# A fused lightning-attention and mixture kernel: values of one chunk with the scores of the next, the state decay on ScalarE, small constants in one tile, another order of the first loads

## Chip, cores and metric

The kernel runs on one core of a Trainium2 chip. The metric is the device time of one execution in microseconds (us); lower is better. Engines are named as in the profile: PE (TensorE matmuls), PEld (its weight loads), DVE (VectorE), ACT (ScalarE), POOL (GpSimd), and SP, whose queue issues most DMAs.

## The reference

First a lightning attention with decay, block by block; then its output, turned to one row per token, goes through four dense experts that are mixed by normalized domain probabilities.

```python
# q, k, v: (4, 8, 768, 64), lam: (8,), blocks of 64 tokens
for b in range(nb):
    intra = (q_b @ k_b.T * Dmask) @ v_b          # Dmask[i, j] = lam ** (i - j), i >= j
    inter = (q_b * lam ** (pos + 1)) @ kv_state
    out_b = intra + inter
    kv_state = lam ** 64 * kv_state + (k_b * lam ** (63 - pos)).T @ v_b
x = out.transpose(0, 2, 1, 3).reshape(3072, 512)
p = probs / (probs.sum(-1) + 1e-9)               # (3072, 4)
y = sum(p[:, e:e+1] * (relu(x @ w1[e]) @ w2[e]) for e in range(4))   # w1: 512x1024, w2: 1024x512
```

All of it is in fp32.

## The kernel before, in words

**Groups and chunks.** The tokens are cut into 24 chunks of 128 (two blocks of 64) with all 8 heads, and the chunks into three groups of 8, numbered 0 to 23. A group of 1024 tokens is what the experts work on. The attention of group 0 runs at the start, between the first expert products; the attention of groups 1 and 2 is spread through the expert products of the group before. `where(n)` gives a chunk its place in the sequence and its batch, and `after_of` the chunk that follows it in the same batch.

**The work of one chunk** is in four functions. `load` brings q, k and v in (SP's queue, L140). `turn` (L590) begins the state, scales k by the decay on POOL (`decayed`, L558), and transposes q and k on PE into two PSUM banks, copied out by ACT; chunks 16 to 23 "come across" instead, their q and k were already laid out in 32x32 blocks by DMAs, and DVE's transpose finishes them (`turn_across`, L575). `scores` (L617) does 32 matmuls of q against k (L633) and up to 32 of k against v for the state (L640), all of 64x64, into two banks `sp`. Three steps for DVE follow: the mask by the decay into `st`, the sum for the second block's state (`middle`), and `end`, which makes the state that the next chunk of the batch starts from: decay (`passed`, L490), then add. `values` (L669) does 32 matmuls of scaled q against the state (L687) and 32 of v against `st` (L705), also 64x64, into two banks, copied out by ACT (L726) with two adds on DVE. After every second chunk POOL makes `pair_sums` (L737), stored to DRAM in `x_blocks`, from which `x_fill` (L352) later refills the seven `xs` tiles of the next group.

**The expert products** are done by a two-level Strassen-like scheme with seven products M1 to M7 on each level. A unit is one group and one expert. In seven steps i of a unit the first product of the next unit (L974, banks g1 and g3, result `m`) and the second product of this unit (L1028, banks q01, q02, q11, q12, result `acc`) run interleaved. In each step the eight slots x hold, in turn, one part of the second product (eight PE matmuls) and two products of the first (four each); the last slot has one. Every bank is emptied by DVE or ACT, often followed by a Relu on ACT (L986).

**The order of work** is written out by hand. A counter `now` counts slots: slot = (unit * 7 + i) * 8 + x. `attention(g)` (L754) puts each chunk's load, turn, scores and values in slots by `BEGIN` (first slot and distance): group 1 turns chunks at 24 + 13i, group 2 at 152 + 22i; scores 4 slots later (6 for chunks that come across), values 10 (12) slots later. DVE work of a chunk goes into the list `lately`, of which one item is taken in each slot after that slot's products (`take`); a `values` forces what it needs of it. POOL's weight sums are `chores`, taken by a model of POOL's time; SP's stores follow from a queue. `FILL` gives the step from which `x_fill` refills one xs tile a step, in slot x = 3. All engines run their own instructions in program order.

**Group 0** has its own list of rows (L1436): turns, scores and values of chunks 0 to 7 (`ts`, `ss`, `vs`) between quarters of the products M1, M2 and M5 of the first unit (L1358), with the loads and POOL's weight sums S1 to S4 (`sum_first`) hung on rows.

**Memory.** Most tiles are 128x512 fp32 from one pool of `NPOOL` = 41 buffers (`small`). PSUM has eight banks: s0, s1 (attention), g1, g3 (first product), q01, q02, q11, q12 (second product). Small constants (`lam_bc`, `probs`, `gate`, `last_gate`, `total`, `decay`) have tiles of their own; of `decay` (128 x 8 x 128) rows 0 to 5 are in use in the attention, and the whole tile is overwritten by gates for the last group.

The lines that matter most:

```python
BEGIN = {1: (24, 13), 2: (8 * 19, 22)}                                        # L751
put(s + (6 if comes_across(n) else 4), lambda n=n: scores(n, ("s0", "s1")))   # L766
put(s + (12 if comes_across(n) else 10), lambda n=n: values(n, ("s0", "s1"))) # L767
tt(eng, o, s, q_decay[:, :, BL - 1:BL].to_broadcast([P, NHP, D]), ALU.mult)   # L491, passed
```

Of the kernel before, what the change touches and what calls it, by code (L numbers as in the profile page):

```python
# [14 lines left out]
FP32 = mybir.dt.float32  # L15
PSUM = bass.MemoryType.PSUM
DRAM = bass.MemoryType.DRAM
NPOOL = 41


@with_exitstack
def kernel(
# [69 lines left out]
    def small(name):  # L92
        return pool.tile([P, W], FP32, name=name, tag="t")
# [7 lines left out]
    def tt(eng, o, a, b, op):  # L101
        eng.tensor_tensor(out=o, in0=a, in1=b, op=op)  # L102
# [308 lines left out]
    def comes_across(n):  # L411
        return where(n)[0] >= SECOND
# [16 lines left out]
            load_across(n)  # L429
            load(n, "k")  # L430

    lam_bc = consts.tile([P, H], FP32, name="lam_bc")
    nc.scalar.dma_start(out=lam_bc[:], in_=lam.partition_broadcast(P))
    for n, names in ((0, "qk"), (1, "qk"), (0, "v"), (1, "v"), (2, "qk")):
        load(n, names)
    raw_w1(0, "A11")
# [21 lines left out]
    decay = consts.tile([P, CPG, P], FP32, name="decay")  # L458
    s_decay = decay[:, 0:4].rearrange("p (r x) (y i) -> p r (x y) i", r=2, i=BL)
    for r in range(2):  # L460
        for ac in range(NHP):
# [26 lines left out]
        tt(nc.vector, by_block(qs), by_block(of), by, ALU.mult)  # L488

    def passed(eng, o, s):  # L490
        tt(eng, o, s, q_decay[:, :, BL - 1:BL].to_broadcast([P, NHP, D]), ALU.mult)  # L491

    probs = consts.tile([P, NTOK // P, E], FP32, name="probs")
    gate = consts.tile([P, NTOK // P, E], FP32, name="gate")
    last_gate = consts.tile([P, CPG * E], FP32, name="last_gate")


    gate_rows = dram.tile([CPG, E, P], FP32, name="gate_rows")
    gate_bc = decay[:]

    def gates():
        total = consts.tile([P, NTOK // P], FP32, name="total")
        nc.vector.reduce_sum(out=total[:], in_=probs[:], axis=AX.X)
        nc.vector.tensor_scalar_add(out=total[:], in0=total[:], scalar1=1e-9)
        nc.vector.reciprocal(out=total[:], in_=total[:])
        nc.vector.tensor_tensor(
            out=gate[:], in0=probs[:], in1=total[:].unsqueeze(2).to_broadcast([P, NTOK // P, E]), op=ALU.mult,
        )

        for i in range(CPG):  # L510
            t = token(LAST, i // 4, i % 4) // P
            nc.vector.tensor_copy(out=last_gate[:, i * E:(i + 1) * E], in_=gate[:, t])

    def turn_gates():
        p, o = bank("s0", "gp"), small("gr")
        n = CPG * E
        nc.tensor.transpose(out=p[0:n, 0:P], in_=last_gate[:], identity=ident[:])
# [99 lines left out]
    def scores(n, tags):  # L617
        all_added()
        while n not in turned:
            take(lately, True)  # L620
        qT, kT = turned[n][0:2]
        while any(f in lately for f in turned[n][3:]):
            take(lately, True)
        begin_state(n)
        kd, vn = nat.pop((n, "kd")), nat[n, "v"]
        first, last = where(n)[0] == 0, where(n)[0] == NCH - 1

        sp = [bank(tags[r], "sp") for r in range(2)]
        blk = [slice(x * BL, (x + 1) * BL) for x in range(2)]
        for ac in range(NHP):  # L630
            for r in range(2):
                for x in range(2):
                    nc.tensor.matmul(  # L633
                        out=sp[r][half[x], ac * BL:(ac + 1) * BL], lhsT=hc(kT)[half[r], ac, blk[x]],
                        rhs=hc(qT)[half[r], ac, blk[x]], start=(ac == 0), stop=True, skip_group_check=True,
                    )
        for ac in range(NHP):
            for x in range(1 if last else 2):
                for r in range(2):
                    nc.tensor.matmul(  # L640
                        out=sp[x][half[r], 256 + ac * D:256 + (ac + 1) * D], lhsT=kd[half[x], 2 * ac + r],
                        rhs=vn[half[x], 4 * r + ac], start=False, stop=True, skip_group_check=True,
                    )
        st = small("st")
        added = [sp[x][:, 256:512].rearrange("p (h d) -> p h d", d=D) for x in range(2)]

        def mask(r):
            tt(
                nc.vector, st[:, r * 256:(r + 1) * 256], sp[r][:, 0:256], s_decay[:, r].rearrange("p h c -> p (h c)"),
                ALU.mult,  # L650
            )

        def middle():
            s = states[n][:, 1]
            if first:
                nc.scalar.copy(out=s, in_=added[0])
            else:
                tt(nc.vector, s, s, added[0], ALU.add)

        def end():  # L660
            s = states[after_of(n)] = small("kv")[:].rearrange("p (x h d) -> p x h d", x=2, d=D)
            passed(nc.vector, s[:, 0], states[n][:, 1])
            tt(nc.vector, s[:, 0], s[:, 0], added[1], ALU.add)

        work = [lambda: (mask(0), mask(1)), middle] + ([] if last else [end])
        soon(n, *work)
        masked[n] = st, work

# [78 lines left out]
            made.add(("blocks", g, x)),  # L747
        ))

    FILL = {1: 18, 2: 43}  # L750
    BEGIN = {1: (24, 13), 2: (8 * 19, 22)}  # L751
    steps = []

    def attention(g):  # L754

        def put(slot, f):
            steps.append((slot, f))

        for i in range(CPG):
            n, s = g * CPG + i, BEGIN[g][0] + BEGIN[g][1] * i  # L760
            put(s - 10, lambda n=n: load_more(n))
            put(s - 6, lambda n=n: load(n, "v"))
            put(s, lambda n=n: turn(n, ("s0", "s1")))
            if comes_across(n):
                put(s - 2, lambda n=n: (decayed(n), nat.pop((n, "k"))))
            put(s + (6 if comes_across(n) else 4), lambda n=n: scores(n, ("s0", "s1")))  # L766
            put(s + (12 if comes_across(n) else 10), lambda n=n: values(n, ("s0", "s1")))  # L767
            if n == 2 * CPG + 3:
                put(s + 17, turn_gates)
        steps.sort(key=lambda s: s[0])  # L770

    def forget():
# [240 lines left out]
    def second_product(g, e, m, banks):  # L1013

        def part(sj, s):
# [20 lines left out]
            if n not in acc:  # L1036
                acc[n] = acc_tile("acc"), set()
            a, begun = acc[n]
            o, x, w = a[:, j * DH:(j + 1) * DH], p[:, s * DH:(s + 1) * DH], gate[:, token(*where_of(n)) // P, e:e + 1]
# [384 lines left out]
        chores.extend((*prepare_w2(0), *(raw[n] for n in ("A11", "A22", "A21"))))  # L1424

    def load_probs():
        nc.scalar.dma_start(out=probs[:], in_=moe_domain_probs.rearrange("(t p) e -> p t e", p=P))

    def loads(*of):
        return lambda: [raw_w1(0, x) if isinstance(x, str) else load(x) for x in of]  # L1430
# [3 lines left out]

    h1, h2 = parts["M1"], parts["M2"]
    for f in (  # L1436
        (ts[0], lambda: warm(3)), (ts[1], lambda: warm(2)), (ss[0], loads(4, 5)), (ss[1], loads("A21", 6)),
        (vs[0], loads("A22")), (vs[1], loads(7)), (ts[2],), (m1[0],), (ss[2],), (m1[2],),
        (vs[2],), (ts[3],), (h2[0][0],), (ss[3],), (ts[4],), (h2[0][1],),
        (vs[3],), (h2[2][0],), (ss[4],), (ts[5],), (h2[2][1], sum_first("S3", "A11", "A21")),  # L1440
        (vs[4],), (h1[1][0],), (ss[5],), (ts[6], sum_first("S1", "A21", "A22", ALU.add)), (h1[1][1],),
        (vs[5],), (h1[3][0],), (ss[6],), (ts[7], load_probs), (h1[3][1], sum_first("S2", "S1", "A11")),
        (vs[6],), (h2[1][0], sum_x(0)), (ss[7],), (h2[1][1], sum_first("S4", "A12", "S2")),
        (begin_chores, m2[3]), (vs[7],), (sum_x(1), quarter_5(0)), (quarter_5(2),),
    ):
        for work in f:
            work()
        now[0] += 1
        pump()
# [178 lines left out]
```

## Time and profile before

| what | value |
|---|---|
| time, three runs | 1174.50, 1175.32, 1175.66 us, median 1175.32 |
| the profiled execution | 1171.55 us |
| its span, first to last instruction | 1169.8 us |
| granted TensorE clock | 1.000 |
| share of the span with PE busy | 99% |
| DVE, ACT, POOL busy | 68%, 23%, 55% |
| DMA moved | 255.63 MB, mean 219 GB/s |

A line of the timeline gives start, length, engine, source line, operation, output<-inputs, shape and count; brackets show idle time of the engine just before and what ended it. Matmuls overlap, and each has a modelled end, so times on PE are best read from start to start. An fp32 matmul of the program stands as two on PE, each with a weight load. A line of the list of waits gives the waiting engine and line, what it waited for, the sum, the number and the longest, in us.

### The profile page before, as it was taken

Reading aid. Unit: us, or ns where it says so; the run is one execution under the profiler, and the core shown is the slowest. Engines: PE = TensorE matmul, PEld = TensorE weight load, DVE = VectorE, ACT = ScalarE, POOL = GpSimd, SP = SyncE. Lnnn points to the kernel's source line nnn. Section 1 sums busy time; section 2 is a strip of 40 time slices with the busy share of each in tenths; the row PEclk is TensorE's granted clock in tenths of the full one; section 3 lists DMA queues with packets and bytes.
Section 4 is the critical chain, followed back from the end, with each engine's and each line's share of the span. In section 5 each row is a group of like instructions: output and inputs, shape, how many; then the busy total and the mean of one; then the engine's idle time right before and its main releaser. Section 6 shows DMA issues by size and latency. Waiting matters only on the chain.

```text
span 1169.8 us, 21185 instructions
## 1 busy us (share of the span) xinstructions
PE 1157.8 (99%) x8095; PEld 1006.5 (86%) x8095; DVE 791.7 (68%) x1407; ACT 271.1 (23%) x540; POOL 646.1 (55%) x640
## 2 busy tenths in 40 slices
PE   8999999999999999999999999999999999999998
PEld 7888888888888888888888888888888888888887
DVE  4666895578478567657747836745775666777785
ACT  4321122112211201211211120221233342341231
POOL 2846327546655761065245215655893683882884
PEclk9999999999999999999999999999999999999999
DMA  9884668998997996787868757785765445354442
GB/s 208 219 257 153 185 195 264 289 315 255 310 334 228 311 277 188 221 264 230 247 195 261 243 182 239 215 278 184 252 212 194 140 152 181 129 182 148 154 180 73
DMA packets 265717, 255.63 MB, mean 219 GB/s; under 512 B 121328, under 2 KB 219408, under 8 KB 265616
## 3 DMA queue, kind: packets, MB, share of 16 engines
q1 hardware_dynamic: 254976, 251.46, 69.0%
q10 hardware_dynamic: 10640, 2.82, 1.1%
q8 instruction: 64, 1.05, 0.4%
q14 instruction: 37, 0.30, 0.1%
HBM read 180.80 MB, written 77.61 MB: 221 GB/s over the span
## 4 chain that ended last, share of the span: by engine, by line
PE 95%; DVE 3%; POOL 1%; issue 0%; DMA 0%; ACTq 0%; ACT 0%; POOLq 0%; DVEq 0%
PE pg L974 39%; PE q L1028 31%; PE pq L1256 13%; PE pM L1358 2%; PE pc L1358 2%; DVE m L102 1%; PE sp L633 1%; PE op L687 1%; PE op L705 1%; PE sp L640 1%; PE qp L603 1%; PE kp L603 1%; POOL acc L102 1%; POOL m L102 1%; DVE sums L102 0%
## 5 line engine op out<-in xcount | busy, mean ns | idle before, releaser
L974 PE MATMUL pg<-xs,ws_in 128*128 128x256 f32 x1960 | 471.6, 380 | 0.8 <-DVE m L102 0.7
L1028 PE MATMUL q<-w2t,m 128*128 128x256 f32 x1792 | 424.4, 380 | 0.0
L974 PEld LDWEIGHTS pg<-xs,ws_in 128*128 128x128 f32 x1960 | 369.8, 190 | 53.7 <-DVE m L102 3.3
L102 DVE TENSOR_TENSOR m<-pg,m 128x512 f32<-128x512 f32 x451 | 307.2, 687 | 120.0 <-PE pg L974 109.8
L1028 PEld LDWEIGHTS q<-w2t,m 128*128 128x128 f32 x1792 | 339.3, 190 | 46.6 <-DVE m L102 0.4
L1046 DVE SCALAR_TENSOR_TENSOR acc<-q,gate,acc 128x256 f32<-128x256 f32 x192 | 92.3, 481 | 126.2 <-PE q L1028 125.7
L102 DVE TENSOR_TENSOR m<-m,m 128x512 f32<-128x512 f32 x184 | 152.5, 829 | 7.7 <-ACT m L986 7.7
L986 ACT ACTIVATE m<-m 128x512 f32<-128x512 f32 x132 | 83.0, 630 | 303.6 <-DVE m L102 302.5
L102 POOL TENSOR_TENSOR m<-m,decay 128x512 f32<-128x512 f32 x64 | 81.8, 1293 | 58.1 <-ACT m L986 44.7
L102 DVE TENSOR_TENSOR sums<-pq,sums 128x256 f32<-128x256 f32 x153 | 64.1, 421 | 45.7 <-PE pq L1256 36.9
L982 ACT COPY m<-pg 128x512 f32<-128x512 f32 x88 | 51.5, 585 | 186.1 <-PE pg L974 176.1
L1256 PE MATMUL pq<-acc,w2t 128*128 128x256 f32 x352 | 86.6, 379 | 0.0
L102 POOL TENSOR_TENSOR xs<-xs 128x256 f32<-128x256 f32 x56 | 44.5, 794 | 73.1 <-DMA xs<-x_blocks 57.4
L1256 PEld LDWEIGHTS pq<-acc,w2t 128*128 128x128 f32 x352 | 66.8, 190 | 9.3 <-issue 0.3
L102 POOL TENSOR_TENSOR to<-xc 128x256 f32<-128x256 f32 x16 | 12.5, 783 | 95.8 <-DVE xc L102 67.8
L102 POOL TENSOR_TENSOR acc<-hT,hT 128x512 f32<-128x512 f32 x32 | 40.2, 1269 | 29.7 <-PE pq L1256 27.8
L102 POOL TENSOR_TENSOR kn<-kn,decay 128x512 f32<-128x512 f32 x16 | 18.0, 1123 | 64.6 <-PE kp L603 43.7
L102 POOL TENSOR_TENSOR w2o<-w2b 128x512 f32<-128x512 f32 x32 | 42.4, 1348 | 18.3 <-DMA w2b<-in_moe_w_dram 10.2
L915 ACT ACTIVATE m<-m 128x512 f32<-128x512 f32 x44 | 27.7, 630 | 106.8 <-DVE m L102 106.8
L102 POOL TENSOR_TENSOR ops<-w2b 128x256 f32<-128x256 f32 x24 | 17.8, 764 | 50.7 <-issue 28.2
L102 POOL TENSOR_TENSOR acc<-hT,acc 128x512 f32<-128x512 f32 x32 | 40.7, 1271 | 7.4 <-PE pq L1256 5.4
L102 POOL TENSOR_TENSOR w2o<-w2b,w2o 128x512 f32<-128x512 f32 x24 | 34.2, 1449 | 5.8 <-issue 4.3
(135 smaller groups left out, 1204.8 us busy)
## 6 DMA issues: line engine op xcount, KB each, us to landing
ws_in<-w_ops SPq DMA_DIRECT2D x70, 896.0 KB, 6.3
w2t<-w_ops SPq DMA_DIRECT2D x66, 256.0 KB, 5.1
w2t<-w_sums SPq DMA_DIRECT2D x64, 256.0 KB, 3.7
w_ops<-ops SPq DMA_DIRECT2D x28, 512.0 KB, 4.3
w2t<-in_moe_w_dram SPq DMA_DIRECT2D x48, 256.0 KB, 3.6
w2b<-in_moe_w_dram SPq DMA_DIRECT2D x32, 256.0 KB, 5.5
w_sums<-w2o SPq DMA_DIRECT2D x16, 512.0 KB, 5.7
w2b<-in_moe_w_dram SPq DMA_DIRECT2D x16, 512.0 KB, 7.6
```

The source lines that it names most:

```text
L102: eng.tensor_tensor(out=o, in0=a, in1=b, op=op)
L603: nc.tensor.transpose(out=x[:, ac * C:(ac + 1) * C], in_=y[:, 2 * ac:2 * ac + 2].rearrange("p r d -> p (r d)"), identity=ident[:],)
L633: nc.tensor.matmul(out=sp[r][half[x], ac * BL:(ac + 1) * BL], lhsT=hc(kT)[half[r], ac, blk[x]], rhs=hc(qT)[half[r], ac, blk[x]], start=(ac ...
L640: nc.tensor.matmul(out=sp[x][half[r], 256 + ac * D:256 + (ac + 1) * D], lhsT=kd[half[x], 2 * ac + r], rhs=vn[half[x], 4 * r + ac], start=F ...
L915: nc.scalar.activation(out=o[:], in_=o[:], func=AF.Relu)
L974: nc.tensor.matmul(out=p[:, j * 256:(j + 1) * 256], lhsT=ws[i][:, j * P:(j + 1) * P], rhs=xs[i], start=(fresh and j == 0), stop=True, skip ...
L982: nc.scalar.copy(out=new[at][:], in_=p[:])
L986: nc.scalar.activation(out=new[at][:], in_=new[at][:], func=AF.Relu)
L1028: nc.tensor.matmul(out=p[:, s * DH:(s + 1) * DH], lhsT=h[A_OF[m]][:, c * 256 + s * P:c * 256 + (s + 1) * P], rhs=fed2[g, e, m][uu][:, c], ...
L1046: nc.vector.scalar_tensor_tensor(out=o, in0=x, scalar=w, in1=o, op0=ALU.mult, op1=ALU.add)
L1256: nc.tensor.matmul(out=p[:, 0:256], lhsT=fed3[e, m, x // 2][:, x % 2, c * P:(c + 1) * P], rhs=b[B_OF[i]][:, c * 256:(c + 1) * 256], start= ...
L1358: nc.tensor.matmul(out=p[:, s * 256:(s + 1) * 256], lhsT=a[c][:, f:f + P], rhs=b[:, c, j * 256:(j + 1) * 256], start=(s == 0 and c == 0 an ...
```

## The change

- **One step for two chunks.** In groups 1 and 2 eleven chunks (12 to 15 and 17 to 23) no longer have their scores alone: `both(n)` runs the values of chunk n-1, in banks s0 and s1, and then at once the scores of chunk n, in banks q02 and q12 of the second product. Chunks 8 to 11 and 16 keep a scores step of their own, and where no step for two follows (8, 9, 10, 15 and 23) values come six slots after the scores. `SCORES` lists the slot of each chunk's scores; the turn is 4 slots ahead (7 for chunks that come across), loads 10 and 6 slots ahead of the turn. `FILL` of group 1 goes from 18 to 19.
- **State decay on ScalarE.** From chunk 8 on `passed` is four ScalarE multiplications of 128x64 by a value per partition, in `end` (there on DVE before) and where a chunk begins (on POOL before).
- **Buffers.** From chunk 8 on the masked scores are written over `kT`; chunks that come across are scaled in place and after their scores. `probs`, `lam_bc`, `last_gate`, `total` and the gates as computed lie in rows 6 and 7 of `decay`; `gate` is kept for two groups, in chunk order, filled by 16 more copies of 128x4. `NPOOL` is 42.
- **First loads.** In group 0's rows chunks 6 and 7 are loaded ahead of the weight blocks A21 and A22, and POOL's sums S1 to S4 come in the later rows, S1 first, with `begin_chores` one row earlier.

```diff
-NPOOL = 41
+NPOOL = 42
...
-    lam_bc = consts.tile([P, H], FP32, name="lam_bc")
+    decay = consts.tile([P, CPG, P], FP32, name="decay")
+    lam_bc = decay[:, 6, 120:128]
...
     def passed(eng, o, s):
+        if eng is nc.scalar:
+            for ac in range(NHP):
+                nc.scalar.mul(out=o[:, ac], in_=s[:, ac], mul=q_decay[:, ac, BL - 1:BL])
+            return
         tt(eng, o, s, q_decay[:, :, BL - 1:BL].to_broadcast([P, NHP, D]), ALU.mult)
...
-        for i in range(CPG):
-            t = token(LAST, i // 4, i % 4) // P
-            nc.vector.tensor_copy(out=last_gate[:, i * E:(i + 1) * E], in_=gate[:, t])
+        for n in range(NG * CPG):
+            t = token(*where_of(n)) // P
+            to = gate[:, n] if n < LAST * CPG else last_gate[:, n % CPG * E:(n % CPG + 1) * E]
+            nc.vector.tensor_copy(out=to, in_=gates_of[:, t])
...
-            passed(nc.gpsimd, states[n][:, 1], states[n][:, 0])
+            passed(nc.gpsimd if n < CPG else nc.scalar, states[n][:, 1], states[n][:, 0])
...
-        qs = small("qs")
-
-        def scaled():
-            scale_q(qs, qT)
-            turned[n] = qT, kT, qs
+        def ready():
+            turned[n] = qT, kT, qT
...
-        soon(n, *(lambda x=x: across(x) for x in (qT, kT)), scaled)
+        soon(n, *(lambda x=x: across(x) for x in (qT, kT)), ready)
...
-        st = small("st")
+        st = small("st") if n < CPG else kT
...
-            passed(nc.vector, s[:, 0], states[n][:, 1])
+            passed(nc.vector if n < CPG else nc.scalar, s[:, 0], states[n][:, 1])
             tt(nc.vector, s[:, 0], s[:, 0], added[1], ALU.add)
 
         work = [lambda: (mask(0), mask(1)), middle] + ([] if last else [end])
+        if comes_across(n):
+            work.append(lambda: scale_q(qT, qT))
...
-    FILL = {1: 18, 2: 43}
-    BEGIN = {1: (24, 13), 2: (8 * 19, 22)}
+    FILL = {1: 19, 2: 43}
+    SCORES = {1: (28, 41, 54, 67, 82, 98, 114, 137), 2: (160, 194, 210, 226, 250, 266, 282, 306)}
+    ALONE = *range(CPG, CPG + 4), 2 * CPG
...
+        def both(n):
+
+            while any(f in lately for f in turned[n][3:]):
+                take(lately, True)
+            values(n - 1, ("s0", "s1"))
+            scores(n, ("q02", "q12"))
+
+        for i, s in enumerate(SCORES[g]):
+            n = g * CPG + i
+            t = s - (7 if comes_across(n) else 4)
+            put(t - 10, lambda n=n: load_more(n))
+            put(t - 6, lambda n=n: load(n, "v"))
+            put(t, lambda n=n: turn(n, ("s0", "s1")))
             if comes_across(n):
-                put(s - 2, lambda n=n: (decayed(n), nat.pop((n, "k"))))
...
+                put(t - 2, lambda n=n: (decayed(n), nat.pop((n, "k"))))
+            if n in ALONE:
+                put(s, lambda n=n: scores(n, ("s0", "s1")))
+            else:
+                put(s, lambda n=n: both(n))
+            if n + 1 in ALONE or i == CPG - 1:
+                put(s + 6, lambda n=n: values(n, ("s0", "s1")))
...
-        (ts[0], lambda: warm(3)), (ts[1], lambda: warm(2)), (ss[0], loads(4, 5)), (ss[1], loads("A21", 6)),
-        (vs[0], loads("A22")), (vs[1], loads(7)), (ts[2],), (m1[0],), (ss[2],), (m1[2],),
+        (ts[0], lambda: warm(3)), (ts[1], lambda: warm(2)), (ss[0], loads(4, 5)), (ss[1], loads(6)),
+        (vs[0], loads(7)), (vs[1], loads("A21", "A22")), (ts[2],), (m1[0],), (ss[2],), (m1[2],),
...
```

More of the change, by code (lines that the diff above doesn't have):

```diff
@@ L430, in load_more @@
             load(n, "k")
-    lam_bc = consts.tile([P, H], FP32, name="lam_bc")
-    nc.scalar.dma_start(out=lam_bc[:], in_=lam.partition_broadcast(P))
+    decay = consts.tile([P, CPG, P], FP32, name="decay")
+    lam_bc = decay[:, 6, 120:128]
+    nc.scalar.dma_start(out=lam_bc, in_=lam.partition_broadcast(P))
     for n, names in ((0, "qk"), (1, "qk"), (0, "v"), (1, "v"), (2, "qk")):
@@ L457 @@
     nc.vector.tensor_tensor(out=blk_ident, in0=ident[:, 0:BL], in1=ident[:, BL:C], op=ALU.add)
-    decay = consts.tile([P, CPG, P], FP32, name="decay")
     s_decay = decay[:, 0:4].rearrange("p (r x) (y i) -> p r (x y) i", r=2, i=BL)
@@ L490, in passed @@
     def passed(eng, o, s):
+        if eng is nc.scalar:
+            for ac in range(NHP):
+                nc.scalar.mul(out=o[:, ac], in_=s[:, ac], mul=q_decay[:, ac, BL - 1:BL])
+            return
         tt(eng, o, s, q_decay[:, :, BL - 1:BL].to_broadcast([P, NHP, D]), ALU.mult)
-    probs = consts.tile([P, NTOK // P, E], FP32, name="probs")
-    gate = consts.tile([P, NTOK // P, E], FP32, name="gate")
-    last_gate = consts.tile([P, CPG * E], FP32, name="last_gate")
+    probs = decay[:, 6, 0:96].rearrange("p (t e) -> p t e", e=E)
+    gates_of = decay[:, 7, 0:96].rearrange("p (t e) -> p t e", e=E)
+    last_gate = decay[:, 7, 96:128]
+    gate = consts.tile([P, LAST * CPG, E], FP32, name="gate")
     gate_rows = dram.tile([CPG, E, P], FP32, name="gate_rows")
@@ L501, in gates @@
     def gates():
[L502 to L505, printed above, removed]
+        total = decay[:, 6, 96:120]
+        nc.vector.reduce_sum(out=total, in_=probs, axis=AX.X)
+        nc.vector.tensor_scalar_add(out=total, in0=total, scalar1=1e-9)
+        nc.vector.reciprocal(out=total, in_=total)
         nc.vector.tensor_tensor(
-            out=gate[:], in0=probs[:], in1=total[:].unsqueeze(2).to_broadcast([P, NTOK // P, E]), op=ALU.mult,
+            out=gates_of, in0=probs, in1=total.unsqueeze(2).to_broadcast([P, NTOK // P, E]), op=ALU.mult,
         )
-        for i in range(CPG):
-            t = token(LAST, i // 4, i % 4) // P
-            nc.vector.tensor_copy(out=last_gate[:, i * E:(i + 1) * E], in_=gate[:, t])
+        for n in range(NG * CPG):
+            t = token(*where_of(n)) // P
+            to = gate[:, n] if n < LAST * CPG else last_gate[:, n % CPG * E:(n % CPG + 1) * E]
+            nc.vector.tensor_copy(out=to, in_=gates_of[:, t])
     def turn_gates():
@@ L516, in turn_gates @@
         n = CPG * E
-        nc.tensor.transpose(out=p[0:n, 0:P], in_=last_gate[:], identity=ident[:])
+        nc.tensor.transpose(out=p[0:n, 0:P], in_=last_gate, identity=ident[:])
         nc.scalar.copy(out=o[0:n, 0:P], in_=p[0:n, 0:P])
@@ L757, in put @@
             steps.append((slot, f))
[L759 to L763, printed above, removed]
-            if comes_across(n):
-                put(s - 2, lambda n=n: (decayed(n), nat.pop((n, "k"))))
-            put(s + (6 if comes_across(n) else 4), lambda n=n: scores(n, ("s0", "s1")))
-            put(s + (12 if comes_across(n) else 10), lambda n=n: values(n, ("s0", "s1")))
+        def both(n):
[9 more added lines that the diff above has]
+            put(t, lambda n=n: turn(n, ("s0", "s1")))
+            if comes_across(n):
+                put(t - 2, lambda n=n: (decayed(n), nat.pop((n, "k"))))
[5 more added lines that the diff above has]
+                put(s + 6, lambda n=n: values(n, ("s0", "s1")))
             if n == 2 * CPG + 3:
-                put(s + 17, turn_gates)
+                put(s + 9, turn_gates)
         steps.sort(key=lambda s: s[0])
@@ L1038, in part @@
             a, begun = acc[n]
-            o, x, w = a[:, j * DH:(j + 1) * DH], p[:, s * DH:(s + 1) * DH], gate[:, token(*where_of(n)) // P, e:e + 1]
+            o, x, w = a[:, j * DH:(j + 1) * DH], p[:, s * DH:(s + 1) * DH], gate[:, n, e:e + 1]
             if e == 0 and j not in begun:
@@ L1426, in load_probs @@
     def load_probs():
-        nc.scalar.dma_start(out=probs[:], in_=moe_domain_probs.rearrange("(t p) e -> p t e", p=P))
+        nc.scalar.dma_start(out=probs, in_=moe_domain_probs.rearrange("(t p) e -> p t e", p=P))
     def loads(*of):
@@ L1436 @@
     for f in (
-        (ts[0], lambda: warm(3)), (ts[1], lambda: warm(2)), (ss[0], loads(4, 5)), (ss[1], loads("A21", 6)),
-        (vs[0], loads("A22")), (vs[1], loads(7)), (ts[2],), (m1[0],), (ss[2],), (m1[2],),
+        (ts[0], lambda: warm(3)), (ts[1], lambda: warm(2)), (ss[0], loads(4, 5)), (ss[1], loads(6)),
+        (vs[0], loads(7)), (vs[1], loads("A21", "A22")), (ts[2],), (m1[0],), (ss[2],), (m1[2],),
         (vs[2],), (ts[3],), (h2[0][0],), (ss[3],), (ts[4],), (h2[0][1],),
[L1440 to L1444, printed above, removed]
+        (vs[3],), (h2[2][0],), (ss[4],), (ts[5],), (h2[2][1],),
+        (vs[4],), (h1[1][0],), (ss[5],), (ts[6],), (h1[1][1],),
+        (vs[5],), (h1[3][0],), (ss[6],), (ts[7], load_probs), (h1[3][1], sum_first("S1", "A21", "A22", ALU.add)),
+        (vs[6],), (h2[1][0], sum_x(0)), (ss[7],), (h2[1][1], sum_first("S2", "S1", "A11"), begin_chores),
+        (m2[3], sum_first("S3", "A11", "A21")), (vs[7],), (sum_x(1), quarter_5(0), sum_first("S4", "A12", "S2")),
+        (quarter_5(2),),
     ):
```

## The prediction

> **What bounds the kernel now.** I read the page first (busy times), then the PE timeline around one chunk, then the list of what PE waited for, then the DVE and ACT timeline at the same places.
>
> ```profile
> span 1169.8 us, 21185 instructions
> PE 1157.8 (99%) x8095; PEld 1006.5 (86%) x8095; DVE 791.7 (68%) x1407; ACT 271.1 (23%) x540; POOL 646.1 (55%) x640
> ...
> q8 instruction: 64, 1.05, 0.4%
> ```
>
> TensorE is busy for 99% of the span, so a gain has two sources only: PE time that is overhead of the small attention matmuls, and about 12 us of PE idle, most of it ahead of 16 us. One chunk, on PE alone:
>
> ```profile
> 134.16 1.89 PE L1028 MATMUL q<-w2t,m 128*128 128x256 f32 x8
> 135.98 0.69 PE L633 MATMUL sp<-qT,kT 64*64 64x64 f32 x32
> 136.49 0.65 PE L640 MATMUL sp<-vn,kn 64*64 64x64 f32 x32
> 137.07 1.13 PE L974 MATMUL pg<-xs,ops 128*128 128x256 f32 x4
> 138.04 1.03 PE L974 MATMUL pg<-xs,w1b 128*128 128x256 f32 x4
> 138.90 1.89 PE L1028 MATMUL q<-w2t,m 128*128 128x256 f32 x8
> ```
>
> Read start to start. Four full matmuls take 0.86 (138.04 to 138.90), so eight take 1.73; here the eight take 1.82, which is 0.09 lost going into the 64x64 tiles. The 64 small ones take 1.09 (135.98 to 137.07). The four after them take 0.97, which is 0.11 lost coming out. A visit costs 0.09 + 1.09 + 0.11 = **1.29 us**. At the start of the kernel two visits follow one another without full matmuls between:
>
> ```profile
> 9.65 0.69 PE L633 MATMUL sp<-qT,kT 64*64 64x64 f32 x32
> 10.16 0.65 PE L640 MATMUL sp<-vn,kd 64*64 64x64 f32 x32
> 10.63 0.65 PE L633 MATMUL sp<-qT,kT 64*64 64x64 f32 x32
> ```
>
> There 64 small matmuls take 0.98 (9.65 to 10.63). So one visit that follows another directly costs 0.31 less. Next, PE's waits and what DVE and ACT do where a chunk's state is updated:
>
> ```profile
> PE op L705 <- issue: 3.1, 2, 2.3
> ...
> PE pg L974 <- DVE xs L102: 0.9, 1, 0.9
> PE pg L974 <- DVE m L102: 0.7, 3, 0.3
> ```
>
> ```profile
> 240.42 0.69 DVE L102 TENSOR_TENSOR m<-pg,m 128x512 f32<-128x512 f32 x1 [0.17 <-PE pg L974]
> 241.03 0.91 DVE L102 TENSOR_TENSOR kv<-kv,decay 128x256 f32<-128x256 f32 x1
> 241.14 0.63 ACT L986 ACTIVATE m<-m 128x512 f32<-128x512 f32 x1 [12.56 <-DVE m L102]
> 241.94 1.89 PE L974 MATMUL pg<-xs,ws_in 128*128 128x256 f32 x8
> 241.97 0.42 DVE L102 TENSOR_TENSOR kv<-kv,sp 128x256 f32<-128x256 f32 x1
> ```
>
> DVE starts on a product 0.17 after PE leaves it: it isn't behind. The decay there (kv<-kv,decay) runs on DVE while ACT is in a Relu. PE hardly waits for DVE.
>
> [...]
>
> **The change, part by part.**
>
> *Values of a chunk with the scores of the next.* Eleven chunks (12 to 15 and 17 to 23) lose a visit of their own: 11 x 0.31 = **-3.4 us**, straight on the path, since PE sets the end. PE runs as many matmuls as before. Bounds: -2.9 if going over to the scores' banks costs 50 ns more each, -3.8 if it costs nothing (the 32 from 10.16 to 10.63 take 0.47, 64 so 0.94, and 1.29 - 0.94 = 0.35).
>
> *The moved slots.* The PE timeline shows stalls at places that now have other neighbours: 0.40 at 251.4 (a chunk's transposes wait for the values three slots before, same banks), 0.39 at 268.7 (DVE late after a decay of 1.10), and 0.8 between 371 and 383 (two transposes and a 1.60 scaling of the first chunk that comes across, in three slots). Now the transposes of a chunk come 4 slots before its step, and a chunk that comes across is scaled after its scores, not before. Of these 1.6 I take **-1.2** (0 to -1.6). Chunks 8 to 11 keep their slots, so what they show stays.
>
> *State decay on ScalarE.* It removes 12 DVE decays (0.43 each, 5 us) and 16 on POOL (0.62 each, 10 us), and adds 28 x 4 = 112 ACTIVATEs of 64 columns. [...] four 128-column copies of L726 took 0.77 in this trace, which is the lower bound[...]. 28 x 1.05 = 29 us on an engine that is 23% busy costs nothing in itself. The 16 that begin a chunk run slots ahead of use; behind them on ACT stand the transposes' copies, due 4 slots later: nothing. The 12 that end a chunk add a wait: DVE's add stands behind the four, they stand behind ACT's Relu of the product just evicted, and behind the add stand DVE's next evictions. After the eviction at 240.42 (done 241.1) the Relu would end at 241.8, the four at 242.8, the add at 243.3, against 242.4 now: DVE is 0.9 later. An evicted bank has 2.6 us (a product of 0.86 and a pair of 1.73) until PE wants it again and DVE uses 0.2 to 1.5 of them, so mostly this stays hidden. Not in three chunks (12, 17, 20; slots 82, 194, 250): their scores lie in q02/q12, and q12 is wanted again six slots on by M2 of the second product. The add that must free it is taken three slots after the step. Counting from PE's end of the last product in that slot: add done at 0.2 + 0.69 + 0.63 + 1.05 + 0.42 + 0.1 = 3.1 us; PE is there after 1.73 + 0.86 = 2.6. That is 0.5 each, **+1.5 us** (0, if the Relu is out of the way, to +3).
>
> *Blocks of instructions.* A joined step has 128 matmuls and 128 weight loads[...] I take **0** (0 to +3).
>
> *Small constants in one tile, one more buffer.* The gates take 24 copies for 8: 16 x 0.08 = 1.3 us of DVE at 69 us. DVE has 1.04 idle at 72.8, and a bank there is wanted again only four quarters of 1.73 later. **0**; without that cover 1.3. Less waiting for buffers helps no PE wait that I see.
>
> *Chunks loaded first.* The transfers of chunks 6 and 7 pass those of A21 and A22 on SP, and the sums S3, S1, S2, S4 on POOL come later and in another order. No PE wait between 16 and 52 us is for a chunk, so nothing is gained. S1 must be there for M5, at 52.1: SP has issued A21 and A22 by 36.9 and a w1 block lands in 5.2, so at about 42; two halves of 1.3 end at about 45. Covered by 7 us. **0** (-0.9 to +1.5[...]).
>
> *Refill of the xs slots* eight slots later (FILL 18 to 19), the last values 18 slots later: 13 slots of 1.62 (seven of 1.73, then one of 0.86) are left to the first use, 21 us, against 6.6 from the issue at 358.4 to POOL's start at 365.1 and 3.7 of POOL. **0**, unless POOL is over 10 us behind.
>
> Sum: -3.4 - 1.2 + 1.5 = **-3.1 us**. The profiled execution took 1171.55, 1.75 more than its span, and would take 1168.4. The runs' median, 1175.32, stands 3.8 above it; I subtract from the median: **1172.2 us**.
>
> **The rivals.**
> 1. *Nothing new in the way:* the Relu and the decay overlap better than priced, so -3.4 - 1.6 = -5.0: 1170.3. For it: DVE is 68% busy and starts within 0.2 of PE. Against: the q12 arithmetic.
> 2. *No difference:* what the joined steps save, PE waits for instructions. Two of the eleven stalls at 1.5 each take the 3.1 back: 1175.3. [...]
> 3. *Slower:* the decay on ACT. If DVE's add comes 1.7 us late instead of 0.9 in all 12, beyond what the banks hide, PE loses about 0.6 each, 7.2: -3.4 - 1.2 + 7.2 = +2.6, 1177.9. It decides from the point where DVE is already 0.8 behind at the add. For it: DVE does masks, sum, add and scaling in four successive slots. Against: DVE's small lag in those windows.
>
> **How the numbers follow.** Forecast 0.50, rival 1 0.15, rival 2 0.18, rival 3 0.17. About 0.2% (2.3 us) is what a measurement of this kernel can tell from no change, so faster begins below 1173.0. The forecast's own width (q12 0 to 3, blocks 0 to 1) is 1170.7 to 1173.7; 0.10 of its 0.50 falls within 0.2%. Faster 0.40 + 0.15 = 0.55, same 0.10 + 0.18 = 0.28, slower 0.17. The range takes in rivals 1 and 2 with the upper bound of the blocks, and leaves out most of 3: 1169.7 to 1176.8.
>
> **What would show it.** In the profile after: eleven steps L687, L705, L633, L640 without full matmuls between, each 2.27 with both switches, where two visits took 2.58; ACT at some 652 instructions, POOL 624, DVE 1411; kv<-kv,decay on ACT at 0.3 each. PE waits "q L1028 <- DVE" of about 0.5 after slots 82, 194, 250 show the bank term right. "issue" stalls inside joined steps would show rival 2, PE pg waits for DVE m of over 3 us in sum rival 3. I am wrong if the joined steps cost more than 2.4 each, or if a wait for x_blocks at the start of group 1 appears.

## The result, and the profile after

| | before | after |
|---|---|---|
| median of nine runs each | 1175.33 us | **1179.58 us** |
| lowest to highest | 1171.54 to 1178.38 | 1178.23 to 1182.80 |
| ratio after/before | | **1.0037**, 95% interval 1.0020 to 1.0053 |
| profiled execution / its span | 1171.55 / 1169.8 | 1181.8 / 1179.7 |

The change makes the kernel slower by 4.2 us. The forecast was 1172.2, the range 1169.7 to 1176.8.

From the head of the profile after:

```profile
PE 1161.3 (98%) x8095; PEld 1008.7 (86%) x8095; DVE 791.0 (67%) x1411; ACT 297.9 (25%) x652; POOL 637.6 (54%) x624
```

The work is what was forecast: DVE 1411, ACT 652, POOL 624, as many matmuls as before. ACT is busier by 26.8 us, which is the decay (29 were forecast); DVE isn't busier, POOL is less so. So the time went into waits. What PE waited for (waiting engine, its operation, releaser; us in total, times, longest):

```profile
PE op L710 <- issue: 4.1, 2, 2.3
PE pg L992 <- DVE m L102: 2.3, 4, 1.1
PE pg L992 <- DVE xs L102: 2.1, 2, 1.4
PE q L1046 <- DVE m L102: 1.6, 2, 1.3
...
PE q L1046 <- DVE kv L102: 0.8, 3, 0.3
```

Before, PE waited 1.6 us for DVE's `m` and `xs`; now it is 6.0, and 0.8 for `kv` (the state). And DVE itself has a new wait, for the four ACTIVATEs of the decay:

```profile
DVE kv L102 <- ACT kv L493: 14.4, 9, 2.5
```

**A joined step** on PE, after:

```profile
270.62 1.89 PE L1046 MATMUL q<-w2t,m 128*128 128x256 f32 x8
272.44 0.69 PE L692 MATMUL op<-qs,kv 64*64 64x64 f32 x32
272.95 0.65 PE L710 MATMUL op<-kT,vn 64*64 64x64 f32 x32
273.42 0.65 PE L636 MATMUL sp<-qT,kT 64*64 64x64 f32 x32
273.89 0.65 PE L643 MATMUL sp<-vn,kn 64*64 64x64 f32 x32
274.46 1.99 PE L992 MATMUL pg<-xs,ws_in 128*128 128x256 f32 x8
276.29 1.89 PE L1046 MATMUL q<-w2t,m 128*128 128x256 f32 x8
```

The 128 small matmuls take 2.02 (272.44 to 274.46), and the eight full ones on each side take 0.1 more than their 1.73: 2.22 in all, where two visits took 2.58. That saves 0.36. In all eleven steps the small matmuls take 2.01 to 2.03, and PE has no wait marked `issue` inside them. This part does what it was said to do.

**Some 8 us after the scores of that same step**, its state is updated. All engines but PE's weight loads, SP and POOL:

```profile
280.99 1.27 DVE L102 TENSOR_TENSOR m<-pg,m 128x512 f32<-128x512 f32 x2
281.70 1.23 ACT L1004 ACTIVATE m<-m 128x512 f32<-128x512 f32 x2 [3.08 <-DVE m L102]
...
282.69 1.03 PE L1046 MATMUL q<-w2t,m 128*128 128x256 f32 x4
282.83 1.05 ACT L493 ACTIVATE kv<-kv,decay 128x64 f32<-128x64 f32 x4
...
283.92 0.42 DVE L102 TENSOR_TENSOR kv<-kv,sp 128x256 f32<-128x256 f32 x1 [1.65 <-ACT kv L493]
284.25 0.68 DVE L102 TENSOR_TENSOR m<-m,m 128x512 f32<-128x512 f32 x1
...
284.99 1.13 PE L1046 MATMUL q<-w2t,m 128*128 128x256 f32 x4 [1.28 <-DVE m L102]
...
286.59 3.67 PE L992 MATMUL pg<-xs,ws_in 128*128 128x256 f32 x8 [0.46 <-DVE m L102]
```

DVE has finished its evictions at 282.26, but its add (283.92) stands behind the decay on ACT, and that behind two Relus of the products just evicted. DVE is idle for 1.65. What it owes next isn't an eviction: it is `m<-m,m` at 284.25, an operand sum of the second product, and PE is at that product already. PE idles 1.28, and 0.46 more at the next product. After that comes something else: the eight matmuls from 286.59 take 3.46 (to 290.05) instead of 1.73. The granted clock of that stretch (PE's busy time and count, then those of PEld, DVE, ACT and POOL, clock, DMA share, GB/s):

```profile
286.70:290.20 3.50, 3.50 (x9) 2.79 (x10) 2.11 (x4) 0.50 (x1) 0.00 (x0) 0.51 1.02 315
```

Half clock for one stretch costs another 1.7 in this execution. It isn't a fixed cost of the change: experiment 2 has the same two stalls in the same place, and its granted clock is 1.000 over the whole profile.

**How parts are compared below.** The first 110 us differ from run to run: in the profile after they hold 3.41 us at half clock (17.09 to 20.50) and two waits of PE marked `issue` (2.29 and 1.85), in that of before full clock and two of 2.31 and 0.80. The 300th full matmul (128x256) begins between 103.9 and 110.6 us in the fourteen profiles of this study. What follows the 3000th takes 432.4 to 432.9 in all of them. So beside the ratio I give the **stretch**, the time in the trace from the start of the 300th full matmul to that of the 3000th, where groups 1 and 2 do their attention: **633.3 before, 638.3 after**. Those 5.0 stand beside the 4.2 of the medians. No other of the fourteen profiles has half clock between those two matmuls, so **638.3 is 636.6 at full clock**, and comparisons below use 636.6. The other 4.8 by which the two first 300 differ (103.9 and 108.7) is scatter: the seven profiles with the new order of first loads reach that matmul at 108.0 on average, the seven with the old order at 108.3. The profile of before was a lucky one, 3.8 under its median.

### The profile page after: what moved, and what is told of

It reads as the page before. It is cut to its first block, busy times and chain, and to the rows that moved or that the text cites. A ratio compares the mean times of both kernels' runs of the same rounds, so it can differ in the third digit from the quotient of the medians.

```text
span 1179.7 us, 21316 instructions
## 1 busy us (share of the span) xinstructions
PE 1161.3 (98%) x8095; PEld 1008.7 (86%) x8095; DVE 791.0 (67%) x1411; ACT 297.9 (25%) x652; POOL 637.6 (54%) x624
## 3 DMA queue, kind: packets, MB, share of 16 engines
q8 instruction: 64, 1.05, 0.4%
## 4 chain that ended last, share of the span: by engine, by line
PE 78%; DVE 5%; POOL 2%; ACT 1%; issue 1%; DMA 0%; POOLq 0%; ACTq 0%; DVEq 0%
PE pg L992 35%; PE q L1046 26%; PE pq L1274 13%; DVE m L102 3%; POOL m L102 1%; PE op L692 1%; PE op L710 1%; PE sp L636 1%; ACT kv L493 1%; PE sp L643 1%; POOL acc L102 1%; POOL ops L102 0%; DVE xs L102 0%; DMA out_dram<-acc 0%; DVE sums L102 0%
## 5 line engine op out<-in xcount | busy, mean ns | idle before, releaser
L924 ACT COPY up<-m 128x512 f32<-128x512 f32 x32 | 18.5, 588 | 78.2 <-DVE m L102 78.1
```

Source lines behind the costliest of these rows:

```text
L924: nc.scalar.copy(out=there[at][:], in_=a[at][:])
```

## The experiments

Each was timed beside the kernel before, on the same chip. "x/before" is the ratio of times with its interval.

**1. Undo the decay on ScalarE where a chunk ends.**

```diff
-            passed(nc.vector if n < CPG else nc.scalar, s[:, 0], states[n][:, 1])
+            passed(nc.vector, s[:, 0], states[n][:, 1])
```

> The changed kernel with one edit: the decay at the end of a chunk on DVE again, as before (the one at a chunk's begin stays on ACT). Theory A (DVE stands idle 1.65 us behind ACT's four multiplications at nine chunk ends, and PE's stalls at 149.7, 253.2, 285.0, 286.6, 453.5, 455.6, 552.2, 581.9 and 584.1 us of the profile come from it): PE gets back about 6 us, and 1.7 more where a stall had led to a stretch at half clock; ratio to the kernel before 0.996 to 0.999. Theory B (the loss lies in the first 100 us, from the other order of loads and sums): it stays at 1.003 to 1.005. Theory C (the joined steps themselves cost more than they save): it stays slower too.

Measured: 1173.02, x/before 0.9985 (0.9971 to 0.9999); stretch 631.6. One line turns the slower kernel into one slightly faster than before: some 6 us of time (0.52%) and 5.0 of stretch at full clock (6.7 with the half clock of the one profile).

**2. Undo the order of group 0's loads and sums alone** (the rows of the list as in the kernel before).

```diff
-        (ts[0], lambda: warm(3)), (ts[1], lambda: warm(2)), (ss[0], loads(4, 5)), (ss[1], loads(6)),
-        (vs[0], loads(7)), (vs[1], loads("A21", "A22")), (ts[2],), (m1[0],), (ss[2],), (m1[2],),
+        (ts[0], lambda: warm(3)), (ts[1], lambda: warm(2)), (ss[0], loads(4, 5)), (ss[1], loads("A21", 6)),
+        (vs[0], loads("A22")), (vs[1], loads(7)), (ts[2],), (m1[0],), (ss[2],), (m1[2],),
...
```

> The changed kernel with one edit: group 0's rows (loads of chunks 6, 7, A21, A22, and POOL's sums S1 to S4) in the order of the kernel before. Theory A (the decay on ACT): at most 1 to 2 us come back, ratio 1.001 to 1.004, and the stalls after 140 us stay. Theory B (the rows: POOL's weight sums run 7 us later and slow DVE's differences of xs at 62 and 94 us): the stall at 62 us goes, that at 94 us is 1.0 and not 1.6, the ones at 97 and 98 us go: 2 us [...]; ratio 1.000 to 1.002.

Measured: 1180.25, x/before 1.0036 (1.0021 to 1.0051), which is the changed kernel's ratio again; stretch 635.6. That is 1.0 under the changed kernel at full clock. The two stalls behind slot 98 are as long as there, but the eight matmuls after them take 1.83 and not 3.46:

```profile
284.29 1.13 PE L1046 MATMUL q<-w2t,m 128*128 128x256 f32 x4 [1.28 <-DVE m L102]
285.89 1.99 PE L992 MATMUL pg<-xs,ws_in 128*128 128x256 f32 x8 [0.47 <-DVE m L102]
287.72 1.89 PE L1046 MATMUL q<-w2t,m 128*128 128x256 f32 x8
```

**3. Both undone.**

> Both edits together: the end decay on DVE and the first rows as before; what is left is the joined steps, the decay at a chunk's begin on ACT, the constants in one tile, and the buffers. If A and B together are the whole loss and each of eleven joined steps saves 0.356 us: 3.9 us less than before and one or two of the old stalls less, ratio 0.994 to 0.997. If the joined steps or the constants cost something of their own (theory C): 0.999 or more.

Measured: 1173.50, x/before 0.9979 (0.9963 to 0.9995); stretch 630.5. Against experiment 1 the rows are worth 1.1 of stretch, with no difference that the times can tell. Against experiment 2 the decay is worth 5.1, without half clock in either profile. The ratio lies between what was expected if the two edits were the whole loss (up to 0.997) and if the joined steps cost something too (0.999 or more).

**4. No joined step, all else as changed.**

```diff
-    ALONE = *range(CPG, CPG + 4), 2 * CPG
+    ALONE = range(CPG, NG * CPG)
```

> The changed kernel with the scores of every chunk in a step of their own (banks s0, s1) and the values six slots later: no joined step, all else as changed. If a joined step saves 0.356 us and costs nothing, this is 3.9 us slower than the changed kernel, ratio to before 1.006 to 1.008. If the banks q02 and q12 cost about 0.4 us at three chunks, 2.6 slower: 1.005 to 1.007. If joined steps don't pay (theory C): no slower than the changed kernel, 1.003 or less.

Measured: 1179.40, x/before 1.0030 (1.0018 to 1.0042); stretch 636.3. Beside the late decay, the joined steps gain next to nothing: 0.3 of stretch at full clock. PE again stands for 1.5 us in the step of slot 98 (at 283.4).

**5. Keep the decay on ScalarE, issue it one slot earlier**, with the piece of work ahead of the add.

```diff
+            if n >= CPG and not last:
+                following(nc.scalar)
 
-        def end():
+        def following(eng):
             s = states[after_of(n)] = small("kv")[:].rearrange("p (x h d) -> p x h d", x=2, d=D)
-            passed(nc.vector if n < CPG else nc.scalar, s[:, 0], states[n][:, 1])
+            passed(eng, s[:, 0], states[n][:, 1])
+
+        def end():
+            if n < CPG:
+                following(nc.vector)
+            s = states[after_of(n)]
             tt(nc.vector, s[:, 0], s[:, 0], added[1], ALU.add)
```

> The changed kernel with the same four ACT multiplications at a chunk's end, but issued one slot earlier, with the sum they wait for; the add on DVE stays where it was. ACT's work is the same, DVE should no longer wait. If the loss is DVE's wait (theory A): within 1.5 us of the kernel with the decay on DVE, 1171.5 to 1174.5 where that had 1173.0, ratio 0.996 to 1.000. If it is what ACT itself does later because of the four (its Relus and copies delayed 1.05 us): it stays at 1.003 or more.

Measured: 1174.38, x/before 0.9993 (0.9977 to 1.0009); stretch 631.0. DVE's wait for ACT's `kv` falls from 14.4 to 1.9. ACT does the same 652 instructions. So it isn't ACT's work that costs, it is that the add follows right behind it.

**6. Decay at the end on DVE, and no joined step.** Edits 1 and 4 together.

> The end decay on DVE, and no joined step (every chunk's scores alone, values six slots later). It tells what joined steps are worth where DVE doesn't wait: if 11 x 0.356 us, 3.9 us slower than the kernel with the decay on DVE alone (1173.0), so 1176 to 1178, ratio 1.000 to 1.003. If joined steps are worth nothing, as beside the ACT decay (1179.4 against 1179.6): 1172 to 1174.

Measured: 1174.68, x/before 0.9996 (0.9977 to 1.0015); stretch 633.0, which is 1.4 over experiment 1. Without the wait for ScalarE the joined steps gain something, though not 3.9.

**7. The kernel before, with the decay at the end on ScalarE and nothing else.**

```diff
     def passed(eng, o, s):
+        if eng is nc.scalar:
+            for ac in range(NHP):
+                nc.scalar.mul(out=o[:, ac], in_=s[:, ac], mul=q_decay[:, ac, BL - 1:BL])
+            return
...
-            passed(nc.vector, s[:, 0], states[n][:, 1])
+            passed(nc.vector if n < CPG else nc.scalar, s[:, 0], states[n][:, 1])
```

> The kernel before with one part of the change alone: the decay at a chunk's end (chunks 8 on) on ACT. The chunks stand in other slots here. Theory A: DVE waits 1.65 us where a Relu is just ahead, at about half of the twelve ends, and PE loses 3 to 7 us: ratio 1.003 to 1.006. If it takes the joined steps or the new slots for the wait to reach PE: 0.999 to 1.001.

Measured: 1175.54, x/before 1.0003 (0.9983 to 1.0023); stretch 635.4. DVE's wait, in this kernel:

```profile
DVE kv L102 <- ACT kv L493: 12.5, 8, 2.5
```

Nearly the whole wait of the changed kernel, at less than half the price: 2.1 of stretch, where taking the decay off ScalarE in the changed kernel saved 5.0. **The same wait of DVE costs by where it falls.** At 583.25 of this trace DVE waits 1.70 and a sum `m<-m,m` stands right behind the add, yet PE loses nothing there: ahead of its next product stands a values step of its own. The plain story that the wait has one price, which expected 3 to 7 us here, began to look too simple.

**8. No decay on ScalarE at all** (edit 1, and the one that begins a chunk on POOL).

```diff
-            passed(nc.gpsimd if n < CPG else nc.scalar, states[n][:, 1], states[n][:, 0])
+            passed(nc.gpsimd, states[n][:, 1], states[n][:, 0])
```

> The changed kernel with no decay on ACT at all: the end's on DVE, the begin's on POOL, as before. If the begin's decay on ACT costs nothing (nobody waits for it for slots): the same as with the end's on DVE alone, 1172 to 1174. If ACT's 1.05 us at a chunk's begin, ahead of its copies of a product or of the transposes, holds PE up (stalls at 181 and 185 us): 1 us less, 1171 to 1173. If POOL and DVE disturb each other more: 1 us more.

Measured: 1174.70, x/before 1.0000 (0.9987 to 1.0013); stretch 631.2, against 631.6 with the begin on ACT: the 16 that begin a chunk cost nothing.

**9. The decay a slot earlier, and group 0's rows as before** (edits 5 and 2).

> The changed kernel with the decay on ScalarE issued one slot ahead of the add, and group 0's order of loads and sums as before. Theory (the wait of the add cost 6.6, the order of group 0 about 1.1 on the stretch from the 300th to the 3000th full matmul): that stretch takes 630 us (before 633.3, with the decay ahead alone 631.0), DVE waits for ACT's kv under 3 us in sum, and the time is 1.0 to 2.0 under the kernel before. Rival (group 0's order costs nothing, what it seemed to cost was scatter of single profiles): the stretch takes 631 or more, no difference to the kernel with the decay ahead alone.

Measured: 1173.54, x/before 0.9978 (0.9962 to 0.9994); stretch 630.6. Against experiment 5 that is 0.4, less than the 1.1 of experiment 3.

**10. The same, with two joined steps moved by six slots.** The profile of experiment 9 still showed PE standing at 280.4, 282.4 and 284.2, behind the joined step of slot 98.

```diff
-    SCORES = {1: (28, 41, 54, 67, 82, 98, 114, 137), 2: (160, 194, 210, 226, 250, 266, 282, 306)}
+    SCORES = {1: (28, 41, 54, 67, 82, 104, 114, 137), 2: (160, 194, 210, 226, 250, 272, 282, 306)}
```

> The kernel before it in this call, with the two joined steps at slots 98 and 266 moved to 104 and 272. Theory (these two stall TensorE because VectorE's work for them comes due together with operand sums of the step they lie in): the stretch from the 300th to the 3000th full matmul loses 0.7 to 1.3 us against the kernel before it in this call, 629 us. Rival (VectorE's work comes late wherever a joined step lies): no difference, the stalls move along by six slots.

Measured: 1170.60, **x/before 0.9960 (0.9944 to 0.9976)**; stretch 629.1. The stalls at 98 are gone and don't move along. One of 0.62 is new, at 476.12, some 3 us after a sum of DVE (472.91) that took 1.55 and not 0.68. This version has the lowest ratio of all; experiments 1, 3, 9 and 12 also lie below the kernel before.

**11. Experiment 9 with no joined step.**

> The first kernel of this call with no joined step: every chunk's values six slots after its scores. It tells what joined steps are worth once the wait for ScalarE is off VectorE's path. Forecast's term (0.31 each, 0.36 as measured on TensorE alone): it is 3.4 to 3.9 us longer than the first kernel of this call on the stretch from the 300th to the 3000th full matmul. Rival (joined steps bunch VectorE's work and give half of it back in stalls): 1.4 to 2.0 longer.

Measured: 1176.45, x/before 0.9998 (0.9978 to 1.0018); stretch 632.3. Joined steps are worth 1.7 against experiment 9, as the rival said, and 3.2 against experiment 10. So what they lose of their 3.9 they lose mostly at slot 98: PE's stalls there are 1.2 in experiment 9 and none in this one; behind slot 266 neither has any.

**12. The changed kernel with the two steps moved, and nothing else.** The decay stays right ahead of the add.

> The changed kernel with the joined steps of slots 98 and 266 at 104 and 272 and nothing else changed: the decay stays right ahead of the add, and group 0's order is the new one. Theory (the add's wait for ScalarE costs wherever VectorE has operand sums behind it): only what the two slots cost goes, 1.5 to 3.5 on the stretch from the 300th to the 3000th full matmul (638.3 in the changed kernel), 635 to 637; DVE still waits 12 us or more for kv, and the time stays at or above the kernel before. Rival (the wait only costs where it meets the crowded slots 98 and 266): the stretch falls to 631 or less, and the time to below the kernel before, as with the decay issued a slot earlier.

Measured: 1173.77, x/before 0.9980 (0.9966 to 0.9994); stretch 631.4. DVE still waits 12.7 for ACT's `kv`, in eight places, and 1.65 at a ninth (447.36) that the list puts down to a DMA.

**My theory fell here.** It held that the wait for ScalarE costs wherever it stands, and expected 635 to 637. DVE waits as long as in the changed kernel, yet this one is faster than the kernel before. The same update of the state, in this kernel:

```profile
287.82 1.89 PE L1046 MATMUL q<-w2t,m 128*128 128x256 f32 x8
288.02 0.69 DVE L102 TENSOR_TENSOR m<-pg,m 128x512 f32<-128x512 f32 x1 [0.17 <-PE pg L992]
288.74 0.63 ACT L1004 ACTIVATE m<-m 128x512 f32<-128x512 f32 x1 [6.27 <-DVE m L102]
289.28 1.05 ACT L493 ACTIVATE kv<-kv,decay 128x64 f32<-128x64 f32 x4
289.55 1.89 PE L992 MATMUL pg<-xs,ws_in 128*128 128x256 f32 x8
290.36 0.42 DVE L102 TENSOR_TENSOR kv<-kv,sp 128x256 f32<-128x256 f32 x1 [1.65 <-ACT kv L493]
290.70 0.48 DVE L1064 SCALAR_TENSOR_TENSOR acc<-q,gate,acc 128x256 f32<-128x256 f32 x1
```

DVE waits the same 1.65, but it had started 0.17 behind PE, one Relu stands ahead of the decay and not two, and what comes after the add are evictions, no operand sums. No wait stands on PE's lines.

## Why the prediction was wrong

**The cause.** Two edits that each cost little cost much together. The stretch in us, in brackets the experiment:

| | slots 98 and 266 | moved to 104 and 272 |
|---|---|---|
| decay right ahead of the add | 636.6 (after, at full clock), 635.6 (2) | 631.4 (12) |
| decay a slot earlier | 631.0 (5), 630.6 (9) | 629.1 (10) |

Experiments 2, 9 and 10 have group 0's rows as before, worth 0.4 to 1.1; the others have the new rows. With equal rows the late decay costs 5.6 (after against 5) and 5.0 (2 against 9) in the changed kernel's slots, and about 2 in the moved ones (2.3 as it stands, the rows in it). The two slots cost 5.2 with the late decay and 1.5 without. The ratios go the same way (1.0037, 0.9980, 0.9993, 0.9960), but with intervals of 0.0015 each way they can't carry the comparison of differences alone. The located waits can. Start to start, PE loses behind the step of slot 98: 0.25 at 281.72, 1.44 at 284.99, 0.63 at 286.59; behind that of slot 266: 0.49 at 581.86 and 1.23 at 584.05. That is 4.0 of the 5.2. Experiment 2 has each of the five again, within 0.02; experiment 12 has none of them, and experiment 5, with the decay a slot earlier, keeps 1.2, all behind slot 98. So of the late decay's 5.6 these two places hold 2.8; most of the rest lies at q12 (1.3), 149.70 (0.85) and 455.62 (0.3), which are told below.

The trace after has its own cross-check. The joined step of slot 210 lies at the same step of a unit and the same place in it as 98 and 266, but no decay and no add follow it there. DVE has operand sums here too:

```profile
478.86 0.68 DVE L102 TENSOR_TENSOR m<-m,m 128x512 f32<-128x512 f32 x1
...
481.76 0.68 DVE L102 TENSOR_TENSOR m<-m,m 128x512 f32<-128x512 f32 x1
482.11 1.89 PE L1046 MATMUL q<-w2t,m 128*128 128x256 f32 x8
...
484.09 1.99 PE L992 MATMUL pg<-xs,ws_in 128*128 128x256 f32 x8
```

Nothing stands in brackets on PE, and the loss at 484.09 is 0.25.

**Point by point.**

*Joined steps, -3.4.* Right: 0.356 each, 3.9, so the upper bound (-3.8, no price for the other banks). What joining saves here is what one visit loses going into the 64x64 tiles and coming out (0.09 + 0.11) and 0.16 within the small matmuls (2.02 for 128, where two visits take 2 x 1.09). What the sum left out is that a joined step also brings DVE the masks, sums and adds of one chunk close to what it owes the products: net 1.7 (9 against 11) in the changed kernel's slots, 0.3 beside the late decay (after against 4).

*Moved slots, -1.2.* Right in what goes: none of the stalls at 251.4, 268.7, 376.1 and 379.2 (1.6 in sum) is left after. But two of 0.4 and 0.2 stand at about 376 and 380 in all five profiles that have the new slots and group 0's old rows (2, 3, 9, 10, 11), so part of this gain hangs on that order. The slots got a credit for their old stalls and no debit for new ones. Nobody asked what DVE does at 98 and 266.

*Decay on ScalarE, +1.5.* **The step that failed**: measured, this term is 5.0 to 5.6. It failed in the words "behind the add stand DVE's next evictions" and "An evicted bank has 2.6 us ... so mostly this stays hidden". The duration was right, though an estimate of mine that no trace of before showed: four take 1.05 (at 282.83 above), one takes 0.33. The three q12 places were right: 0.43 each at 253.23, 453.48 and 552.18, all still there in experiment 12, 1.3 in sum against 1.5. One of them, after:

```profile
252.76 0.42 DVE L102 TENSOR_TENSOR kv<-kv,sp 128x256 f32<-128x256 f32 x1 [1.65 <-ACT kv L493]
...
253.23 1.99 PE L1046 MATMUL q<-w2t,m 128*128 128x256 f32 x8 [0.26 <-DVE kv L102]
```

The lateness was short: idle 1.65 less the 0.43 of a decay that DVE no longer does is 1.2, not 0.9 (the place it was read from, 241.03, had a slow decay of 0.91). And the cover was the wrong one for the other places: behind the add stand also operand sums, the differences `xs` (0.85 at 149.70, in experiments 2, 4, 7 and 12 too) and the scaling of q. A sum that PE needs next has no bank to hide behind. Without the late decay the change gains 1.7 to 2.3 of stretch (experiments 1 and 5).

*Instructions, 0.* This was an estimate of mine, as was rival 2: a wait marked `issue` names no cause, so no profile shows what PE lacks there. Right for the joined steps: none has such a wait. Of the two long ones ahead of 50 us the second is 1.05 longer than before (1.85 at 48.31, 0.80 at 45.46), in the part of the kernel that scatters. *Constants and gates, refill of xs: 0.* No wait after points to either; they were not tried alone.

*Chunks loaded first, 0.* A little low: 0.4 to 1.1 of stretch. The 7 us of cover for S1 held, but POOL's later work moved too. Stalls of 0.2 at 180.96 and 0.8 at 185.32 (the second behind DVE's `m`) are in every profile with the new rows and in none with the old, against the 0.6 at 376 and 380 named above.

*Rival 3* had the mechanism, with too large a size (+7.2 against 5.0 to 5.6), and its condition, "from the point where DVE is already 0.8 behind at the add", is what slots 98 and 266 fulfil. Its sign, over 3 us of PE's pg waits for DVE's `m`, came to 2.3 as written; 1.6 more stand on the other product's line (q). It spread the price evenly over twelve places; half of it sits in two. Its "against", DVE's small lag, was read at the windows of before, while the steps were about to be moved to others. That is why it got 0.17.

What stays open: about 1.0 of the 5.0 by which the stretch of the one profile is longer. The wanted terms are -3.9 and -1.6; found against them are 4.0 (98 and 266), 1.7 (half clock), 1.3 (q12), 0.85 (xs at 149.70), 0.3 at 455.62, 1.0 (rows), and 0.25 at 484.09.

## What to carry to other kernels

When an instruction of one engine is put behind another engine's, list what stands behind it in that queue and when each is due, at every place where it occurs: an eviction may have a bank's time to spare, an operand that the next product reads has none. Price edits that move steps and edits that add waits together, in the new places. And where the cost turns out to be a wait, issue its cause a slot earlier or move the step: each of these one-line edits recovered the loss here (0.9993 and 0.9980 from 1.0037), and with group 0's order put back as well, both together gave the fastest of the versions tried (0.9960). Last, look at the clock before a difference of single profiles is read: one interval at half clock makes 1.7 of the 6.7 that experiment 1 seems to win.

## What the runs showed of the hardware

- In the profile after the clock is at half for 3.41 us twice, from 17.09 to 20.50 and from 286.74 to 290.15, and at full between. In the 3.41 us ahead of each PE is busy for 1.56 and 1.67; the second of these (283.32 to 286.74) holds both stalls behind slot 98. In the profile before, 3.41 us with PE busy for 1.75 (10.92 to 14.33) are followed by full clock. Experiment 2 has the same stalls, a clock of 1.000, and 1.83 for the eight matmuls behind them. That the stalls brought the half clock on is my reading of these places; what decides it was not shown.
- Four ACTIVATEs of 64 columns in a row take 1.05 (282.83 in the profile after), yet DVE behind them loses 1.65 (283.92): the Relus queued ahead of them on ACT (two in 1.23, at 281.70) count too.
- Some of DVE's work takes longer while POOL works, as the expectations of experiments 2 and 8 suppose: in the profile after four differences `xs<-xs` of 128x256 take 5.71 at 92.45, with POOL busy for 5.63 of them, and 1.80 at 149.13, with POOL idle.
